# A decode kernel with two attention layers: parts of three query weight blocks loaded through the GpSimd queue onto chosen partitions

## The chip, the cores and the metric

The kernel runs on one core of a Trainium2 chip. The metric is the time on the device in microseconds; three runs of the kernel before gave 1343.22, 1343.85 and 1345.13, so the median is 1343.85.

## The reference

One token of width 640 goes through an attention layer with a key and value cache, a two-layer MLP, and then through both again with the same weights and the same cache.

```python
B, Sq, D = 1, 1, 640
H, Sk, Dh = 32, 8192, 128
def _A_ref(x, k_cache, v_cache, wq, wo):
    q = (lambda x, *d: x.transpose(*d))((x @ wq).reshape(B, Sq, H, Dh), 0, 2, 1, 3)
    scores = jnp.einsum("bhqd,bhkd->bhqk", q, k_cache) * (Dh ** -0.5)
    p = _softmax(scores, axis=-1)
    o = jnp.einsum("bhqk,bhkd->bhqd", p, v_cache)
    return (lambda x, *d: x.transpose(*d))(o, 0, 2, 1, 3).reshape(B, Sq, H * Dh) @ wo
...
x = x + _A_ref(_layernorm(x, axis=-1), A_k_cache, A_v_cache, A_wq, A_wo)
x = x + _B_ref(_layernorm(x, axis=-1), B_w1, B_w2)
x = x + _A_ref(_layernorm(x, axis=-1), A_k_cache, A_v_cache, A_wq, A_wo)
x = x + _B_ref(_layernorm(x, axis=-1), B_w1, B_w2)
```

All data are float32. Each of the 32 heads has 4 MB of keys and 4 MB of values, and both attention layers read them all, apart from a few pieces that stay on the chip between the layers.

## The kernel before

The work is a stream of loads. The keys and values are cut into units of up to 6 MB (`UNITS`, laid out in host memory in `kv` in the order of `ORDER`), and each unit is one transfer over all 128 partitions from SyncE's queue into `ring`, a buffer of 34,000 columns in which `place` looks for room. `pump` (L179) issues the next units while there is room, and is called each time that `release` gives a piece back, which is after the last matmul that reads it. So SyncE issues a load when PE has finished with an older one, and two to three loads are always queued ahead of PE.

PE, VectorE and ScalarE work head by head: scores (L516), the largest of them (L531, L536, L537), the exponentials (L545), four transposes (L552), values (L570), and the sum over the blocks (L587 to L604). Four heads are a group, eight groups a layer. In layer 2 the heads run in another order (`HEADS[1]`). Inside the program the layers are `L` = 0 and 1; this text calls them layer 1 and layer 2. Groups are counted by `k` from 0.

Between the pieces of a head's scores and values `side_work` slips in steps of two queues, `chores` and `slow`. A generator there says for which engine its next step is. Two of them matter here. `run_out(k)` is queued when group k + 1 begins; it projects the outputs of group k with `wo` and then calls `load_wo`, which fetches from ScalarE's queue (L280) the output weights of group k + 1 and the query weights of group k + 2 in one transfer of 2560 KB into `both_t`: 2560 columns of query weights, five row blocks of 512, and 2560 of output weights. `queries_of(k + 1)` is queued with the third head of group k; it runs `wide_queries` (L435): five matmuls (L440), one for each block of 128 of the 640 rows, that spread over four strips of the array, and then for each of the four heads a row scaled by VectorE (L452) and one matmul that sums the strips (L454). So the query weights are asked for with the first head of a group and used with its third.

The order of the instructions on each engine is that in which the Python code emits them (`manual_schedule`); waits between engines and for transfers are put in by the framework from what each instruction reads and writes. Transfers from one kind of queue share eight semaphores in turn, so that a ninth transfer waits for the first to be complete.

At the end of layer 1 the next layer's first units are placed in `mix`, `wct` and the region `by_parts` (`ring` beyond the units, L142), which holds `w2` at the end of each layer; the last loads of a layer are parts of `w2`. The buffer `by_parts` has 4480 columns; between the ends of the layers units reach 2880 columns into it, and the other 1600 lie unused.

Of the kernel before, what the change touches and what calls it, by code (L numbers as in the profile page):

```python
# [10 lines left out]
F32 = mybir.dt.float32  # L11
# [4 lines left out]
P = 128  # L16
D = 640
H = 32
SK = 8192
DH = 128  # L20
DFF = 1728
EPS = 1e-5
NB = D // P
HG = 4
NG = H // HG
# [62 lines left out]
RING = 4248  # L88
WC_AT = [5, 8]
MIX_AT = [[7, 9, 11, 13], [12, 16, 20, 24]]  # L90
FLAT = 3072
EDGE = 4096
BIG = 1536
# [30 lines left out]


@with_exitstack
def decode_kernel(ctx: ExitStack, tc: tile.TileContext, x, kv, wq, wo, wqo, w1, w2, out):
    nc = tc.nc
    consts = ctx.enter_context(tc.tile_pool(name="consts", bufs=1))
    wts = ctx.enter_context(tc.tile_pool(name="wts", bufs=1))  # L130
# [7 lines left out]

    ring = consts.tile([P, 8 * (RING + W2_UNITS)], F32, name="ring")
    by_parts = ring[:, 8 * RING :]  # L142
# [8 lines left out]
    dram_at, o = {}, 0  # L151
# [119 lines left out]
    wo_t = both_t[:, HG * D :].rearrange("p (j d) -> p j d", d=D)  # L271

    def load_wq(g, queue):
        queue.dma_start(both_t[:, : HG * D], wq[P * g : P * g + P])

    def load_wo(L, k, queue):

        g = GROUPS[L][k]
        if 0 < k < NG - 1:
            queue.dma_start(both_t, wqo[L, k - 1])  # L280
# [132 lines left out]
    def queries(g, xc, r):  # L413

        pq = side
        for c in range(NB):
            for j in range(HG):
                nc.tensor.matmul(
                    pq[32 * j : 32 * j + 32, :DH],
                    xc[:, c : c + 1].to_broadcast([P, 32]),  # L420
                    wq_t[:, c, j * DH : (j + 1) * DH],
                    start=(c == 0),
                    stop=(c == NB - 1),
                )
        yield "dve"
        row = work.tile([P, DR], F32, name="q_row")[:, :DH]
        nc.vector.tensor_scalar(row, pq[:, :DH], r[0], SCALE, op0=ALU.mult, op1=ALU.mult)
        yield "pe"
        pt = side
        nc.tensor.matmul(pt[:, :HG], row, sel[:, :HG], start=True, stop=True)  # L430
        yield "dve"
        qT[g] = work.tile([P, HG], F32, name="qT", bufs=2)
        nc.vector.tensor_copy(qT[g], pt[:, :HG])

    def wide_queries(g, xc, r):  # L435

        pq = side
        for c in range(NB):
            strip = c % 4
            nc.tensor.matmul(  # L440
                pq[32 * strip : 32 * strip + 32],
                xc[:, c : c + 1].to_broadcast([P, 32]),
                wq_t[:, c],
                start=c < 4,
                stop=c in (1, 2, 3, 4),
                skip_group_check=True,
            )
# [246 lines left out]
    def attention_and_mlp(L, xr, s, before=None):  # L694
# [25 lines left out]
                    queue.pop(0)  # L720

        def queries_of(k):
            yield from wide_queries(groups[k], xc, r)

        def run_out(k):

# [51 lines left out]
        def due(h):  # L778
# [105 lines left out]
    def mlp(L, o, last, xp, ph):  # L884
# [128 lines left out]
        for c in range(NB):  # L1013
# [1 line left out]
            nc.tensor.matmul(  # L1015
                pq[32 * g : 32 * g + 32, :DH],
                cols[:, c : c + 1].to_broadcast([P, 32]),
                wq_t[:, c, (HG - 1) * DH :],
                start=c < 4,
                stop=c in (1, 2, 3, 4),  # L1020
                skip_group_check=True,
# [44 lines left out]
def _laid_out(A_x, A_k_cache, A_v_cache, A_wq, A_wo, B_w1, B_w2):  # L1066
# [24 lines left out]
    wq = np.asarray(A_wq).reshape(NB, P, NG, HG * DH).transpose(2, 1, 0, 3).reshape(NG, P, HG * D)  # L1091
    wo = np.asarray(A_wo)[:, _COLS].reshape(NG, HG, DH, D).transpose(0, 2, 1, 3)
    wqo = [
        [np.concatenate([wq[b], wo[a].reshape(P, HG * D)], 1) for a, b in zip(gs[1:-1], gs[2:])]
        for gs in GROUPS
# [16 lines left out]
                for loads in W2_LOADS  # L1112
            ]
        ),
    }


# [22 lines left out]
```

## Time and profile before

| What | Value |
|---|---|
| Median of three runs | 1343.85 us |
| Span of the profiled execution, from the first to the last instruction | 1340.6 us |
| Between the span and the median | 3.25 us |
| TensorE matmul busy | 874.0 us, 65% |
| VectorE busy | 290.2 us, 22% |
| ScalarE busy | 62.6 us, 5% |
| GpSimd busy | 2.9 us, 10 instructions |
| Read from memory | 570.83 MB, 426 GB/s over the span |

The page lists of the profiled execution its span; the time around it is taken as the difference to the median of the runs. The lines of the page that matter are shown in the prediction. In a line of the page's fifth part stand the line of the program, the engine, the operation, output and input, how often; then busy time in us and the mean of one in ns; then the idle time of the engine just before, and what ended it. In a window's line the last two numbers are the mean busy share of the 16 DMA engines and what they moved.

### The profile page before, as it was taken

How to read it: one execution, taken by the hardware profiler on the slowest of the kernel's cores; microseconds unless marked ns; L12 is line 12 of the kernel's file. 1: busy time of each engine (PE TensorE's matmuls, PEld its weight loads, DVE VectorE, ACT ScalarE, POOL GpSimd, SP SyncE). 2: the span in 40 equal slices, each digit the busy share in tenths (PEclk: the TensorE clock that was granted, in tenths of full speed). 3: DMA queues.
4: the chain of work that ended last, by engine and by line, in shares of the span. 5: the costliest groups of instructions: out<-in, count | busy, mean ns of one | idle time of the engine just before them, and what ended most of it. 6: DMA issues, size and time to landing. Idle time of an engine off the chain costs nothing.

```text
span 1340.6 us, 13403 instructions
## 1 busy us (share of the span) xinstructions
PE 874.0 (65%) x5806; PEld 255.5 (19%) x5806; DVE 290.2 (22%) x956; ACT 62.6 (5%) x155; POOL 2.9 (0%) x10
## 2 busy tenths in 40 slices
PE   5463575767657656676688755657566666567687
PEld 2110121111111111112243211112111111111123
DVE  2120121211212112223123212221221212212222
ACT  0000000000000000000000000000000000000000
POOL 0000000000000000000000000000000000000000
PEclk8686787988777887788799977887778787888789
DMA  9999999999999999999999999999999999999998
GB/s 395 431 435 430 442 423 437 429 428 437 432 434 429 428 439 426 433 425 415 425 396 425 430 435 433 432 433 431 433 429 434 432 428 433 437 427 436 425 424 333
DMA packets 24546, 571.70 MB, mean 426 GB/s; under 512 B 2724, under 2 KB 2984, under 8 KB 6952
## 3 DMA queue, kind: packets, MB, share of 16 engines
q1 hardware_dynamic: 21464, 529.31, 92.1%
q10 hardware_dynamic: 3024, 41.53, 7.3%
q8 instruction: 46, 0.75, 0.2%
q14 instruction: 12, 0.10, 0.0%
HBM read 570.83 MB, written 0.00 MB: 426 GB/s over the span
## 4 chain that ended last, share of the span: by engine, by line
DMA 67%; PE 27%; DVE 4%; ACT 1%; issue 1%; SPq 0%; ACTq 0%; DVEq 0%
DMA ring<-in_kv 66%; PE ps L516 10%; PE outs L570 9%; PE side L672 1%; DMA ring<-in_w 1%; DVE p L591 1%; PE acc L621 1%; PE side L440 1%; ACT p L545 1%; DVE h_t L531 1%; PE small L536 1%; PE small L604 1%; PE side L454 1%; DVE p L552 0%; DVE h_t L537 0%
## 5 line engine op out<-in xcount | busy, mean ns | idle before, releaser
L516 PE MATMUL ps<-ring,spread_q 128*32 128x512 f32 (+3 forms) x2088 | 332.7, 727 | 149.2 <-DMA ring<-in_kv 148.6
L570 PE MATMUL outs<-ring,p 128*4 128x512 f32 (+3 forms) x2080 | 310.6, 732 | 164.1 <-DMA ring<-in_kv 95.7
L531 DVE TENSOR_REDUCE h_t<-ps 128x1 f32<-128x512 f32 x64 | 44.3, 691 | 365.4 <-PE ps L516 365.4
L570 PEld LDWEIGHTS outs<-ring,p 128*4 128x4 f32 x2080 | 50.6, 95 | 348.4 <-issue 233.8
L516 PEld LDWEIGHTS ps<-ring,spread_q 128*32 128x32 f32 x2088 | 63.9, 124 | 277.5 <-issue 188.8
L545 ACT ACTIVATE p<-ps,h_t 128x512 f32<-128x512 f32 x63 | 43.3, 687 | 1161.2 <-DVE h_t L537 1161.2
L552 DVE STREAM_TRANSPOSE p<-p 128x128 f32<-128x128 f32 x256 | 79.8, 312 | 63.9 <-ACT p L545 57.2
L587 DVE TENSOR_SCALAR p<-outs,ind 128x128 f32<-128x128 f32 x64 | 22.5, 351 | 317.2 <-PE outs L570 317.2
L604 PE MATMUL small<-ones,p 128*128 128x1 f32 (+1 forms) x128 | 25.3, 267 | 97.4 <-DVE p L591 97.4
L591 DVE SCALAR_TENSOR_TENSOR p<-outs,ind,p 128x128 f32<-128x128 f32 x188 | 66.0, 351 | 6.7
L536 PE MATMUL small<-ident,h_t 128*128 128x128 f32 x128 | 32.7, 339 | 40.1 <-DVE h_t L531 39.9
L604 PEld LDWEIGHTS small<-ones,p 128*128 128x128 f32 x128 | 19.9, 195 | 159.7 <-DVE p L591 158.9
L672 PE MATMUL side<-w_t,wct 128*128 128x448 f32 (+1 forms) x80 | 45.3, 651 | 0.0
L452 DVE TENSOR_SCALAR q_row<-side,ln_r 128x128 f32<-128x128 f32 x56 | 19.5, 349 | 106.0 <-PE ps L516 59.0
L440 PE MATMUL side<-both_t,ln_xc 128*32 128x512 f32 x140 | 37.3, 844 | 0.0
L536 PEld LDWEIGHTS small<-ident,h_t 128*128 128x128 f32 x128 | 20.0, 196 | 89.0 <-DVE h_t L531 85.5
L621 PE MATMUL acc<-both_t,o_cols 128*64 128x320 f32 x220 | 34.6, 458 | 0.0
L454 PEld LDWEIGHTS side<-sel,q_row 128*128 128x128 f32 x112 | 19.3, 216 | 56.3 <-DVE q_row L452 29.9
L537 DVE TENSOR_REDUCE h_t<-small 128x1 f32<-128x128 f32 x64 | 18.7, 292 | 35.4 <-PE small L536 35.4
L454 PE MATMUL side<-sel,q_row 128*128 128x1 f32 x112 | 24.1, 284 | 0.3 <-DVE q_row L452 0.2
L621 PEld LDWEIGHTS acc<-both_t,o_cols 128*64 128x64 f32 x220 | 15.5, 147 | 29.4 <-issue 17.7
L672 PEld LDWEIGHTS side<-w_t,wct 128*128 128x128 f32 x80 | 13.5, 211 | 32.4 <-issue 32.4
(148 smaller groups left out, 219.5 us busy)
## 6 DMA issues: line engine op xcount, KB each, us to landing
ring<-in_kv SPq DMA_DIRECT2D x50, 6144.0 KB, 35.0
ring<-in_kv SPq DMA_DIRECT2D x23, 4096.0 KB, 33.2
ring<-in_kv SPq DMA_DIRECT2D x29, 2048.0 KB, 27.7
both_t<-in_wqo ACTq DMA_DIRECT2D x12, 2560.0 KB, 24.7
ring<-in_kv SPq DMA_DIRECT2D x4, 5120.0 KB, 34.6
ring<-in_kv SPq DMA_DIRECT2D x9, 1024.0 KB, 23.9
w_t<-in_w ACTq DMA_DIRECT2D x1, 4320.0 KB
ring<-in_kv SPq DMA_DIRECT2D x5, 768.0 KB, 29.5
```

Of the source, the lines that this page charges most:

```text
L440: nc.tensor.matmul(pq[32 * strip : 32 * strip + 32], xc[:, c : c + 1].to_broadcast([P, 32]), wq_t[:, c], start=c < 4, stop=c in (1, 2, 3, ...
L454: nc.tensor.matmul(mine[:, :1], row, one_of_each, start=True, stop=True, skip_group_check=True)
L516: nc.tensor.matmul(hd.ps[32 * g : 32 * g + 32, c : c + n], spread_q[:, 3 - r : 35 - r], tile_of[:, at + g * n : at + (g + 1) * n], start=f ...
L531: nc.vector.tensor_reduce(hd.nm, hd.ps, AX.X, ALU.max, negate=True)
L536: nc.tensor.matmul(pt[:, :P], hd.nm.to_broadcast([P, P]), ident, start=True, stop=True)
L545: nc.scalar.activation(hd.p, hd.ps, AF.Exp, bias=hd.low, scale=scale, accum_out=hd.l)
L552: nc.vector.transpose(hd.all_p[:, b * P : (b + 1) * P], hd.p[:, b * P : (b + 1) * P])
L570: nc.tensor.matmul((hd.out if r0 < 2 else hd.out_2)[32 * g : 32 * g + 4, r0:r1].rearrange("p r d -> p (r d)"), hd.all_p[:, 32 * i : 32 * i ...
L591: nc.vector.scalar_tensor_tensor(oc, hd.out[:, r], ind[:, r : r + 1], oc, op0=ALU.mult, op1=ALU.add)
L604: nc.tensor.matmul(pt[:, :n], part, mask.to_broadcast([P, n]), start=i == 0, stop=i == len(parts) - 1,)
L621: nc.tensor.matmul(acc[64 * g : 64 * g + 64, : 2 * DR], col.to_broadcast([P, 64]), wt[:, 2 * DR * g : 2 * DR * (g + 1)], start=first, stop ...
L672: nc.tensor.matmul(pt[:, :n], wct[:, c], w1_t[:, c, f : f + n], start=(c == 0), stop=(c == NB - 1),)
```

## The change

Three pieces of query weights leave the transfer of `load_wo` and come through the GpSimd queue instead: two of five row blocks (3 and 4) of the weights that are loaded at k = 2, in both layers, and one row block (4) of those loaded at k = 4 in layer 2. A row block is 128 rows of 512 columns, 256 KB. The other transfer from ScalarE's queue starts at a later column and is shorter by as much; to that end the row blocks are stored in the order 3, 4, 0, 1, 2 (`POS`).

The rows that leave are laid on some of the partitions only: 0 to 11, 16 to 19, 28 to 31, 32 to 43, 48 to 51, 60 to 67, 92 to 99 and 124 to 127 for the first, and a part of these for the second. Each such partition holds up to five rows (`slots`) of 512 columns beside each other. A slot is 520 columns wide, and the slots take the first 1024 (or 512) columns of `both_t`, which is now the end of `ring`, and the unused columns of `by_parts` ahead of it. That area is set to zero once at the start.

The table `loads` lists the transfers: the number of DMA engines each is meant to use, the first partition, the number of partitions, and the slots; with 0 slots it moves a few words into the unused columns between slots. The access patterns are cut so that the outermost sizes of both sides have that number as common divisor. The numbers of one round, 3, 1, 1, 2, 1, 1, 6, 1, add up to 16.

For the matmul the rows of a slot need the matching elements of the normalized input as a column. `early_columns`, queued as a slow step with head 4 of each layer, makes these columns: two matmuls bring blocks 3 and 4 of the input into rows, VectorE sets a row in `mix` to zero and copies the pieces to their places, five or eight matmuls turn them into columns, and one copy keeps them in `early_x`. `wide_queries` then has three or four matmuls of the ordinary kind, and five or three with a slot as weights and the column of `early_x`; elements for partitions that hold no such row are zero.

```diff
+POS = {4: 0, 3: 1, 0: 2, 1: 3, 2: 4}
+SLOT = HG * DH + 8
+GAP = 64
+EARLY = {
+    2: dict(
+        chunks=[3, 4],
+        slots=5,
+        held=[
+            (5, [(0, 12), (16, 4), (28, 4), (48, 4), (60, 8), (92, 8), (124, 4)]),
+            (3, [(32, 12)]),
+        ],
+        loads=[
+            (3, 0, 12, 5),
+            (1, 12, 4, 0),
+            (1, 16, 4, 5),
+            (2, 20, 8, 0),
+            (1, 28, 4, 5),
+            (1, 96, 4, 5),
+            (6, 68, 24, 0),
+            (1, 92, 4, 5),
+            (3, 32, 12, 3),
+            (1, 12, 4, 0),
+            (1, 48, 4, 5),
+            (2, 20, 8, 0),
+            (2, 60, 8, 5),
+            (6, 68, 24, 0),
+            (1, 124, 4, 5),
+        ],
+    ),
+    4: dict(
+        chunks=[4],
+        slots=3,
+        held=[
+            (3, [(0, 12), (16, 4), (28, 4), (60, 8), (92, 4)]),
+            (2, [(32, 12), (96, 4)]),
+        ],
+        loads=[
+            (3, 0, 12, 3),
...
+            (7, 68, 28, 0),
+        ],
+    ),
+}
+EARLY_IN = [[2], [2, 4]]
...
-    both_t = wts.tile([P, 2 * HG * D], F32, name="both_t")
+    both_t = ring[:, both_at:]
...
+    def load_early(L, k):
+
+        spec = EARLY[k]
+        for i, load in enumerate(spec["loads"]):
+            engines, first, rows, slots = load
+            pieces, n = split(load)
...
+            source = early[o:o_end].rearrange("(g m) -> g m", g=pieces)[:, :n]
+            where = slots_of(spec)[first : first + rows]
...
+            nc.gpsimd.dma_start(where, source)
...
-            queue.dma_start(both_t, wqo[L, k - 1])
+            n = HG * DH * len(EARLY[k]["chunks"]) if k in EARLY_IN[L] else 0
+            queue.dma_start(both_t[:, n:], wqo[L, k - 1, :, n:])
+            if k in EARLY_IN[L]:
+                load_early(L, k)
             return
...
+    nc.vector.memset(ring[:, both_at - 8 * 200 : both_at], 0.0)
...
-    def wide_queries(g, xc, r):
+    def wide_queries(g, xc, r, k=None):
 
         pq = side
-        for c in range(NB):
+        parts = [(xc[:, c : c + 1], wq_t[:, POS[c]]) for c in range(NB)]
+        if k in early_x:
+            spec = EARLY[k]
+            parts = [p for c, p in enumerate(parts) if c not in spec["chunks"]]
+            parts += [
+                (early_x[k][:, s : s + 1], slots_of(spec)[:, s, : HG * DH])
+                for s in range(spec["slots"])
+            ]
+        for c, (column, weights) in enumerate(parts):
...
+            if where == 4:
+                slow.append([early_columns(L, xc), "pe"])
```

On PE, in layer 1, the third head of group 2 computes the queries of group 3, whose weights are the first to come in two parts. Before:

```order
L604 MATMUL small<-ones,p 128x1 [waits DVE_49]
L516 MATMUL ps<-ring,spread_q 32x512 [waits DMAHW6_49,PE_49]
L516 MATMUL ps<-ring,spread_q 32x512 x3
L440 MATMUL side<-both_t,ln_xc 32x512 [waits DMAHW4_49,Activation_49]
L440 MATMUL side<-both_t,ln_xc 32x512 x4
L516 MATMUL ps<-ring,spread_q 32x512 x4
L454 MATMUL side<-sel,q_row 128x1 [waits DVE_49]
```

The same place with the change, where the line numbers have moved (L613 was L440, L689 was L516):

```order
L777 MATMUL small<-ones,p 128x1 [waits DVE_49]
L689 MATMUL ps<-ring,spread_q 32x512 [waits DMAHW6_49,PE_49]
L689 MATMUL ps<-ring,spread_q 32x512 x3
L613 MATMUL side<-ring,ln_xc 32x512 [waits DMAHW4_49,Activation_49]
L613 MATMUL side<-ring,ln_xc 32x512 x2
L613 MATMUL side<-ring,early_x 32x512 [waits DMASW5_49,DMASW6_49,DMASW4_49,DMASW7_49,DMASW2_49,DMASW0_49]
L613 MATMUL side<-ring,early_x 32x512 x4
L689 MATMUL ps<-ring,spread_q 32x512 x4
L627 MATMUL side<-sel,q_row 128x1 [waits DVE_49]
```

Two of the five query matmuls have gone, and five come behind the other three; the first of these waits for transfers of the GpSimd queue (DMASW), ahead of the head's remaining scores. On GpSimd, which before had only the four powers of the layer norms, these transfers stand for k = 2 in layer 1:

```order
L461 TENSOR_TENSOR ln_r<-ln_v,mhalf 128x1 [waits DVE_49]
L392 DMA ring<-in_early 12x5x512 [waits DMAHW5_49,DMAHW4_49,PE_49]
L392 DMA ring<-in_early 4x3x4
L392 DMA ring<-in_early 4x5x512
L392 DMA ring<-in_early 8x1x4
L392 DMA ring<-in_early 4x5x512 x2
L392 DMA ring<-in_early 24x1x4
L392 DMA ring<-in_early 4x5x512
L392 DMA ring<-in_early 12x3x512 [waits DMASW0_49]
L392 DMA ring<-in_early 4x3x4 [waits DMASW1_49]
L392 DMA ring<-in_early 4x5x512 [waits DMASW2_49]
L392 DMA ring<-in_early 8x1x4 [waits DMASW3_49]
```

The first eight follow each other without a wait; from the ninth on each waits until an earlier one is complete. On VectorE, the steps of `early_columns` in layer 1 come behind the two of `run_out(0)`:

```order
L906 RECIPROCAL rl_g<-small 128x4 [waits PE_49]
L907 SCALAR_TENSOR_TENSOR o_cols<-o_cols,rl_g 128x4 [waits DVE_49]
L578 MEMSET mix 32x640
L587 COPY mix<-side 32x5x12 [waits DVE_49,PE_49]
L587 COPY mix<-side 32x5x4 x3
L587 COPY mix<-side 32x5x8 x2
L587 COPY mix<-side 32x5x4
L587 COPY mix<-side 32x3x12
L594 COPY early_x<-side 128x5 [waits PE_49]
L704 TENSOR_REDUCE h_t<-ps 128x1 [waits PE_49]
```

Before, the largest of the scores (L531, now L704) followed at once.

More of the change, by code (lines that the diff above doesn't have):

```diff
@@ new lines, with placed, filled @@
+EARLY_IN = [[2], [2, 4]]
+def placed(spec):
+    o = 0
+    for slots, runs in spec["held"]:
+        n = sum(m for _, m in runs)
+        for first, m in runs:
+            yield slots, first, m, o, n
+            o += m
+        o += (slots - 1) * n
+def filled(spec):
+    at = np.full((spec["slots"], P), -1)
+    for slots, first, m, o, n in placed(spec):
+        for s in range(slots):
+            for i in range(m):
+                c, d = divmod(o + s * n + i, P)
+                at[s, first + i] = P * spec["chunks"][c] + d
+    held = np.sort(at[at >= 0])
+    assert (held == np.concatenate([P * c + np.arange(P) for c in spec["chunks"]])).all()
+    loaded = np.zeros((spec["slots"], P), bool)
+    for _, first, rows, slots in spec["loads"]:
+        loaded[:slots, first : first + rows] = True
+    assert loaded[at >= 0].all()
+    return at
@@ L91, with split @@
+def split(load):
+    engines, _, rows, slots = load
+    pieces = engines if engines > 1 else slots or 3
+    n = rows * (slots * HG * DH if slots else 12 if engines == 1 else 4)
+    return pieces, n // pieces
+EARLY_AT, _o = {}, 0
+for _L in range(2):
+    for _k in EARLY_IN[_L]:
+        for _i, _load in enumerate(EARLY[_k]["loads"]):
+            EARLY_AT[_L, _k, _i] = _o
+            _pieces, _n = split(_load)
+            _o += _pieces * (_n + GAP)
+EARLY_SIZE = _o
 FLAT = 3072
@@ L722, in queries_of @@
         def queries_of(k):
-            yield from wide_queries(groups[k], xc, r)
+            yield from wide_queries(groups[k], xc, r, k - 1)
         def run_out(k):
@@ L1090, in _laid_out @@
     w2[W2_LAST:, -1, : D // 2] = w2[:W2_LAST, -1, D // 2 :]
-    wq = np.asarray(A_wq).reshape(NB, P, NG, HG * DH).transpose(2, 1, 0, 3).reshape(NG, P, HG * D)
+    order = sorted(POS, key=POS.get)
+    wq = np.asarray(A_wq).reshape(NB, P, NG, HG * DH)[order].transpose(2, 1, 0, 3).reshape(NG, P, HG * D)
+    early = np.zeros(EARLY_SIZE, wq.dtype)
+    for k, spec in EARLY.items():
+        at = filled(spec)
+        for L in (L for L in range(2) if k in EARLY_IN[L]):
+            cols = HG * DH * GROUPS[L][k + 1]
+            rows = np.zeros((spec["slots"], P, HG * DH), wq.dtype)
+            rows[at >= 0] = np.asarray(A_wq)[at[at >= 0], cols : cols + HG * DH]
+            for i, load in enumerate(spec["loads"]):
+                _, first, count, slots = load
+                if slots:
+                    pieces, n = split(load)
+                    block = early[EARLY_AT[L, k, i] :][: pieces * (n + GAP)].reshape(pieces, n + GAP)
+                    held = rows[:slots, first : first + count].transpose(1, 0, 2)
+                    block[:, :n] = held.reshape(pieces, n)
     wo = np.asarray(A_wo)[:, _COLS].reshape(NG, HG, DH, D).transpose(0, 2, 1, 3)
@@ L1114, in _laid_out @@
         ),
+        "early": early,
     }
```

76 lines of the change are left out of this document (67 added, 9 removed).

## The prediction

> **What bounds the kernel now.** I read the page first: the span, the DMA slices, the queues, the chain that ended last and the two largest groups of PE.
>
> ```profile
> span 1340.6 us, 13403 instructions
> ...
> DMA  9999999999999999999999999999999999999998
> GB/s 395 431 435 430 442 423 437 429 428 437 432 434 429 428 439 426 433 425 415 425 396 425 430 435 433 432 433 431 433 429 434 432 428 433 437 427 436 425 424 333
> ...
> q1 hardware_dynamic: 21464, 529.31, 92.1%
> q10 hardware_dynamic: 3024, 41.53, 7.3%
> q8 instruction: 46, 0.75, 0.2%
> ...
> DMA 67%; PE 27%; DVE 4%; ACT 1%; issue 1%; SPq 0%; ACTq 0%; DVEq 0%
> ...
> L516 PE MATMUL ps<-ring,spread_q 128*32 128x512 f32 (+3 forms) x2088 | 332.7, 727 | 149.2 <-DMA ring<-in_kv 148.6
> L570 PE MATMUL outs<-ring,p 128*4 128x512 f32 (+3 forms) x2080 | 310.6, 732 | 164.1 <-DMA ring<-in_kv 95.7
> ```
>
> The reader is to see that the 16 DMA engines are busy from end to end (92.1 + 7.3 + 0.2 = 99.6% of their time) at some 430 GB/s, and that PE waits for ring data 148.6 + 95.7 = 244 us in all. So added PE or DVE work is covered as long as it stays far below that, and time falls only if the engine that finishes last has less to move. The slice with 333 GB/s is the last one, so next I cut the end into windows (busy time of the engines, PE clock, then the DMA share and GB/s).
>
> ```profile
> core 0: us, PE busy (x) PEld busy (x) DVE busy (x) ACT busy (x) POOL busy (x), PEclk, DMA share, GB/s
> 1330.00:1331.00 1.00, 1.00 (x8) 0.94 (x8) 0.61 (x4) 0.37 (x2) 0.00 (x0) 1.00 1.00 399
> 1331.00:1332.00 1.00, 0.74 (x21) 0.63 (x25) 0.17 (x1) 0.00 (x0) 0.00 (x0) 1.00 0.83 334
> 1332.00:1333.00 1.00, 1.00 (x36) 0.96 (x32) 0.00 (x0) 0.00 (x0) 0.00 (x0) 1.00 0.58 242
> 1333.00:1334.00 1.00, 1.00 (x30) 0.71 (x20) 0.08 (x2) 0.00 (x0) 0.00 (x0) 1.00 0.59 242
> 1334.00:1335.00 1.00, 0.99 (x26) 0.76 (x25) 0.87 (x6) 0.00 (x0) 0.00 (x0) 1.00 0.49 197
> 1335.00:1336.00 1.00, 0.81 (x19) 0.59 (x15) 0.23 (x3) 0.00 (x0) 0.15 (x1) 1.00 0.37 133
> 1336.00:1337.00 1.00, 0.96 (x28) 0.39 (x20) 0.00 (x0) 0.00 (x0) 0.40 (x1) 1.00 0.02 8
> ```
>
> A share of 0.58 is 9.3 of 16 engines. Seven engines run out at about 1331.6 (the 0.17 missing in that window is 2.7 us of engine time, 0.4 us for each of seven); nine go on, the last to about 1336.3. The sum of what is missing from 1331 to 1336.3 is 0.17 + 0.42 + 0.41 + 0.51 + 0.63 + 0.28 = 2.4 us of all engines: more than that, less the cost of small pieces, no redistribution can win there. The change's table names seven engines that get weights (0 to 2, 4, 7, 8, 15) and passes over nine, so the count fits. The q8 row shows instruction fetches as one load that need not be even: 0.2% of 16 engines is 43 us, 4.8 us each on nine. The page doesn't name the engines.
>
> Layer 1 has the same unevenness, seen where the queue runs dry.
>
> ```profile
> 636.00:637.00 1.00, 0.00 (x0) 0.00 (x0) 0.00 (x0) 0.00 (x0) 0.00 (x0) 1.00 0.80 302
> 637.00:638.00 1.00, 0.94 (x16) 0.42 (x16) 0.00 (x0) 0.00 (x0) 0.00 (x0) 1.00 0.91 272
> ...
> 690.00:693.00 3.00, 2.23 (x24) 1.39 (x24) 0.88 (x3) 0.37 (x1) 0.00 (x0) 1.00 0.88 359
> 693.00:694.00 1.00, 1.00 (x12) 0.92 (x15) 0.50 (x4) 0.37 (x2) 0.00 (x0) 1.00 0.85 223
> 694.00:695.00 1.00, 1.00 (x33) 0.96 (x36) 0.17 (x1) 0.00 (x0) 0.00 (x0) 1.00 0.74 280
> ```
>
> Missing here: 0.20 + 0.09 + 0.36 + 0.15 + 0.26 = 1.06 us.
>
> **The change, part by part.** *Bytes moved between engines.* In layer 1 512 KB of weights leave the even load, in layer 2 768 KB. Each engine loses a sixteenth, 32 and 48 KB. At 430/16 = 27 GB/s that is 1.2 and 1.8 us. Seven engines get the bytes back in pieces of 2 KB: 256 in layer 1, 388 in layer 2 (132 for the third block, four of them spare). The nearest rate for small rows is the window from 1335 (rows of 1.25 to 5 KB): 133/(0.37·16) = 22.5 GB/s, so 91 ns a piece against 76 ns at full rate. In layer 2 each of the seven carries 52 to 64 pieces, 4.7 to 5.8 us, less the 1.8 removed: 2.9 to 4.0 later. The seven then end at about 1331.6 + 2.9 = 1334.5 to 1335.6, the nine at 1336.3 − 1.8 = 1334.5. The end comes 0.7 to 1.8 us earlier; I take **−1.4**, where most of the seven meet the nine. In layer 1 the bound from above is the 1.06 us that is missing, from below nothing, since part of it is waiting for the issue of the next load; I take **−0.7**.
>
> *PE and DVE.* The next rows price the added work.
>
> ```profile
> L440 PE MATMUL side<-both_t,ln_xc 128*32 128x512 f32 x140 | 37.3, 844 | 0.0
> ...
> 1.84 0.48 DVE L323 MEMSET outs<- 128x512 f32 x1
> ...
> 6.66 0.32 DVE L1041 TENSOR_REDUCE x_s<-xr 128x1 f32<-128x160 f32 x1 [4.24 <-DMA xr<-in_x]
> ```
>
> One pass of a query matmul costs 37.3/140 = 0.27 us. Two passes each, three matmuls more for a group with five slots: 1.6 us twice; two more for the third block: 1.1 us. The columns for them (7 and 10 short matmuls, 8 and 14 small DVE copies) come once a layer. All of it lies in PE's 244 us of waiting and costs **0**; without that cover it would be some 8 us. The memset of 1600 columns, 1.5 us by the row of 512, fits into the 4.24 us for which DVE waits for `x`.
>
> *Small transfers and their reports.* 42 transfers on a queue that the kernel didn't use, seventeen of them only to move the choice of engine on. No row prices their reports; below by nothing, above by the 91 ns of a 2 KB piece for each on each engine, 42 · 0.09 = 3.8 us. Most are a few bytes, so I take **+0.2**, and one more instruction fetch may add to one engine, +0.2 on average.
>
> *The wait that is added.* The query matmul of a group now waits for the early pieces, and everything of PE stands behind it. When do they land?
>
> ```profile
> ring<-in_kv SPq DMA_DIRECT2D x50, 6144.0 KB, 35.0
> ...
> both_t<-in_wqo ACTq DMA_DIRECT2D x12, 2560.0 KB, 24.7
> ...
> 205.14 0.33 ACTq L280 DMA_DIRECT2D both_t<-in_wqo  x1
> ...
> 247.64 1.45 PE L440 MATMUL side<-both_t,ln_xc 128*32 128x512 f32 x9
> ...
> 846.49 0.33 ACTq L280 DMA_DIRECT2D both_t<-in_wqo  x1
> ...
> 883.90 2.37 PE L440 MATMUL side<-both_t,ln_xc 128*32 128x512 f32 x9
> ...
> 1011.23 0.34 ACTq L280 DMA_DIRECT2D both_t<-in_wqo  x1
> ...
> 1055.58 2.77 PE L440 MATMUL side<-both_t,ln_xc 128*32 128x512 f32 x9
> ```
>
> The time from issue to use is 42.5, 37.4 and 44.4 us. A ring row of 48 KB takes an engine 1.8 us, a weight row of 20 KB 0.76 us. The weights alone would need 6 us but land after 24.7: 8 · (1.8 + 0.76) = 20.6 us and the ends. So an engine alternates between the two queues row by row, and the price of the new queue is its number of turns, 1.8 us each. If a turn takes all that one transfer has for an engine, there are 15 transfers and so some 17 turns: nine beside the weights at 2.6 us, eight at 1.9, 39 us, about on time. A PE that comes 4 us late costs nothing, because loads are queued:
>
> ```profile
> 244.87 25.77 DMA ring<-in_kv
> ...
> 257.00 0.33 SPq L189 DMA_DIRECT2D ring<-in_kv  x1
> ...
> 863.95 40.46 DMA ring<-in_kv
> ...
> 887.64 0.33 SPq L189 DMA_DIRECT2D ring<-in_kv  x1
> ```
>
> The load issued at 244.87 lands at 270.6, and SP's next issue, which PE releases, comes at 257.0: 11.6 us of slack with 2 us for a start (904.4 − 887.6 − 2 = 14.8 in layer 2). Landings up to some 53 us after issue cost **0**. I take this case, being nearest to the 24.7 us row.
>
> Sum: −1.4 − 0.7 + 0.4 = −1.7 us on the span of 1340.6. The median of the runs, 1343.85, is 3.25 above the span, and that part stays: **1342.1 us**.
>
> **Rivals.** *Two pieces or one to a turn (slower).* If the new queue gives an engine one piece of 2 KB a turn, the engines with 40 pieces need 40 + 15 = 55 turns, 23 + 46 · 1.9 = 110 us; two at a time 35 turns, 73 us. PE then stands at the query until the ring queue is empty and the pieces have the engines alone. From 53 us on each group costs idle DMA. In layer 1 the queue is empty at 270.6; PE then takes 9.4 us (257.0 − 247.6) to the next release and the load 2 us to start: 11. In layer 2: 3.7 + 2, 6. Two at a time: +17, **1359 us** (the third block, 14 to 24 turns, is still in time). One at a time: the third block costs some 9 as well (between the other two), and in each of the three some 25 pieces are still left (2.3 us) and the second batch, which waits for the first one's reports, has to start (2 us), 4 each: 17 + 9 + 12 = +38, **1380 us**. For it speaks the row-by-row turn of the other queues; against it that those rows are whole rows, and the trace has no transfer of many pieces. The Trainium skill, "DMA: Bandwidth & Descriptors", section "Queues, rings and completion order", says that an engine drains a whole packet, typically 9 to 17 descriptors, before it changes rings; by that the forecast holds. The same page's section "SWDGE vs HWDGE vs iDMA" has a packet preferably at most 4096 B, which would be two pieces and 1359 us. No row here decides between them.
>
> *Other engines than named (no effect, or slower).* If the pieces are dealt to all engines, nothing is gained and 644 · 15 ns / 16 = 0.6 us lost: **1344 us**; if they fall on late engines, 2.9 us and 1.7 us are added: 1348. For it: the engine follows only from the order of the transfers. Against: the counts 3+1+1+2+1+1+6+1 make 16. The Trainium skill, same page, section "Why a DMA increments its semaphore by 16 and not by 1", tells of such an exception for some direct copies of that queue.
>
> **Numbers.** Forecast (right engines, in time) 0.55, own range 1340.6 to 1343.6. Other engines 0.10, two pieces a turn 0.15, one piece 0.20. The range takes in all but the last: 1340.6 to 1361. A measurement here tells about 0.2%, 2.7 us. Faster (below 1341.2): 0.15, the good end of the forecast. Within: 0.40 of the forecast and 0.05 of the other engines, 0.45. Slower: 0.40.
>
> **What would show it.** Right: in the last windows the DMA share stays near 1 until some 1334 and falls within 2 us; the early pieces' matmul follows the three others of its group with under 5 us of idle PE; no DMA slice in either layer drops below 400 besides the first and the last. Wrong: a wait of PE of 20 us or more at the query with DMA windows near 0 behind it (pieces per turn), or shares of 0.58 for 4 us at the end as now (engines).

## The result, and the profile after

The changed kernel takes 1395.71 us, the median of four runs (1392.38 to 1400.56); the kernel before takes 1343.96 us. The ratio is 1.039, with a 95% interval of 1.0368 to 1.0412. The prediction, 1342.1 us with a range up to 1361, was wrong.

The profiled execution took 1396.84 us. These are its lines on the page:

```profile
span 1395.1 us, 13619 instructions
...
DMA  9999999769999999999999999969999979999997
GB/s 398 434 435 431 428 425 424 316 262 431 432 428 441 427 436 426 432 426 418 429 388 429 430 430 431 424 248 403 432 429 427 426 308 434 433 430 433 429 424 328
DMA packets 28883, 571.75 MB, mean 410 GB/s; under 512 B 6738, under 2 KB 6998, under 8 KB 11288
...
q1 hardware_dynamic: 21464, 529.31, 88.9%
q0 software_dynamic: 4336, 1.36, 0.4%
q10 hardware_dynamic: 3024, 40.22, 6.8%
...
L613 PE MATMUL side<-ring,early_x 128*32 128x512 f32 x26 | 9.1, 1059 | 77.7 <-DMA ring<-in_early 77.7
```

Four slices of the DMA row have fallen (316 and 262, 248, 308 GB/s), in three places, and PE waits 77.7 us for the early pieces. The timeline has PE's three waits in brackets, with their ends in the first column, and SyncE's first load after the first of them:

```profile
280.21 2.74 PE L613 MATMUL side<-ring,early_x 128*32 128x512 f32 x9 [32.26 <-DMA ring<-in_early]
...
291.83 9.31 SPq L287 DMA_DIRECT2D ring<-in_kv  x2
...
937.83 2.74 PE L613 MATMUL side<-ring,early_x 128*32 128x512 f32 x9 [27.47 <-DMA ring<-in_early]
1117.67 1.07 PE L613 MATMUL side<-ring,early_x 128*32 128x512 f32 x3 [17.93 <-DMA ring<-in_early]
```

In windows (busy times, then PE's granted clock, DMA share and GB/s), first around each wait and then within the first:

```profile
260.00:300.00 40.00, 16.05 (x92) 4.67 (x96) 5.32 (x17) 0.78 (x2) 3.32 (x5) 0.66 0.46 181
920.00:950.00 30.00, 10.07 (x56) 3.25 (x60) 3.60 (x11) 0.78 (x2) 3.33 (x5) 0.61 0.47 178
1110.00:1130.00 20.00, 10.23 (x48) 2.82 (x48) 3.60 (x11) 0.78 (x2) 0.00 (x0) 0.59 0.60 237
...
270.00:275.00 5.00, 0.00 (x0) 0.00 (x0) 0.00 (x0) 0.00 (x0) 2.60 (x4) 0.50 0.13 22
280.00:285.00 5.00, 4.79 (x24) 1.39 (x28) 0.35 (x1) 0.00 (x0) 0.00 (x0) 0.62 0.00 0
285.00:290.00 5.00, 3.12 (x23) 1.15 (x22) 2.10 (x6) 0.78 (x2) 0.00 (x0) 1.00 0.01 2
```

The idle DMA time is 40 · 0.54 = 21.6, 30 · 0.53 = 15.9 and 20 · 0.40 = 8.0 us, 45.5 us in all. In layer 1 the loads that were queued have run out soon after 270; the last pieces land at 280, and PE, whose clock has fallen to 0.50 while it waited, needs until 291.8 to release the next load. The rest is in the queues' shares: q1, q10, q0 and q8 (0.2%) are 96.3% of 1395.1 us = 1343.5 us, and were 99.6% of 1340.6 = 1335.2. So 45.5 us idle and 8.3 us more of work make 53.8 of the 54.5 us by which the span grew.

GpSimd's timeline shows that it asked early. The transfers of k = 2 in layer 1 start at 165.27, as soon as the previous queries are done, while the ordinary weights are asked for 40 us later:

```profile
165.27 2.92 POOL L392 DMA_DIRECT2D ring<-in_early  x4 [154.55 <-PE ps L689]
189.83 0.72 POOL L392 DMA_DIRECT2D ring<-in_early  x1 [21.63 <-issue]
...
271.27 2.60 POOL L392 DMA_DIRECT2D ring<-in_early  x4 [19.08 <-issue]
275.83 0.72 POOL L392 DMA_DIRECT2D ring<-in_early  x1 [1.96 <-issue]
```

From the first issue to PE's start it is 280.21 − 165.27 = 115 us here, and by the same rows 110 us in layer 2 (issue at 827.42) and 102 us for the third block (1015.66). Between its issues GpSimd stands for up to 23.6 us for nothing that the profile names.

### The profile page after: what moved, and what is told of

Same layout as the page of the kernel before. It is cut to its first block, busy times and chain, and to the rows that moved or that the text cites. A ratio compares the mean times of both kernels' runs of the same rounds, so it can differ in the third digit from the quotient of the medians.

```text
span 1395.1 us, 13619 instructions
## 1 busy us (share of the span) xinstructions
PE 885.5 (63%) x5856; PEld 261.1 (19%) x5856; DVE 295.8 (21%) x984; ACT 62.5 (4%) x155; POOL 31.1 (2%) x52
## 2 busy tenths in 40 slices
DMA packets 28883, 571.75 MB, mean 410 GB/s; under 512 B 6738, under 2 KB 6998, under 8 KB 11288
## 3 DMA queue, kind: packets, MB, share of 16 engines
q1 hardware_dynamic: 21464, 529.31, 88.9%
q0 software_dynamic: 4336, 1.36, 0.4%
## 4 chain that ended last, share of the span: by engine, by line
DMA 48%; PE 26%; issue 17%; DVE 4%; another core or an unknown queue 2%; POOL 1%; ACT 1%; SPq 0%; ACTq 0%; POOLq 0%; DVEq 0%
DMA ring<-in_kv 44%; PE outs L743 10%; PE ps L689 9%; PE side L613 2%; DMA ring<-in_wqo 1%; DVE p L764 1%; POOL ring L392 1%; DMA ring<-in_w 1%; DVE h_t L704 1%; PE side L845 1%; ACT p L718 1%; PE small L709 1%; PE acc L794 1%; PE small L777 1%
## 5 line engine op out<-in xcount | busy, mean ns | idle before, releaser
L743 PE MATMUL outs<-ring,p 128*4 128x512 f32 (+3 forms) x2080 | 318.1, 748 | 158.4 <-DMA ring<-in_kv 92.5
L689 PE MATMUL ps<-ring,spread_q 128*32 128x512 f32 (+3 forms) x2104 | 330.6, 714 | 117.6 <-DMA ring<-in_kv 117.1
L704 DVE TENSOR_REDUCE h_t<-ps 128x1 f32<-128x512 f32 x64 | 44.3, 691 | 336.2 <-PE ps L689 336.2
L689 PEld LDWEIGHTS ps<-ring,spread_q 128*32 128x32 f32 x2104 | 65.5, 123 | 248.1 <-issue 179.1
L625 DVE TENSOR_SCALAR q_row<-side,ln_r 128x128 f32<-128x128 f32 x56 | 19.5, 349 | 184.3 <-PE side L613 75.9
L613 PE MATMUL side<-ring,early_x 128*32 128x512 f32 x26 | 9.1, 1059 | 77.7 <-DMA ring<-in_early 77.7
L777 PEld LDWEIGHTS small<-ones,p 128*128 128x128 f32 x128 | 19.5, 192 | 157.8 <-DVE p L764 156.9
L392 POOL DMA_DIRECT2D ring<-in_early x42 | 28.2, 674 | 589.1 <-PE ps L689 332.6
L794 PE MATMUL acc<-ring,o_cols 128*64 128x320 f32 x220 | 35.6, 469 | 0.0
L613 PE MATMUL side<-ring,ln_xc 128*32 128x512 f32 x130 | 33.9, 838 | 0.0
L627 PE MATMUL side<-sel,q_row 128*128 128x1 f32 x112 | 24.5, 288 | 0.4 <-DVE q_row L625 0.2
```

Source lines behind the costliest of these rows:

```text
L613: nc.tensor.matmul(pq[32 * strip : 32 * strip + 32], column.to_broadcast([P, 32]), weights, start=c < 4, stop=c >= len(parts) - 4, skip_gr ...
L627: nc.tensor.matmul(mine[:, :1], row, one_of_each, start=True, stop=True, skip_group_check=True)
L689: nc.tensor.matmul(hd.ps[32 * g : 32 * g + 32, c : c + n], spread_q[:, 3 - r : 35 - r], tile_of[:, at + g * n : at + (g + 1) * n], start=f ...
L704: nc.vector.tensor_reduce(hd.nm, hd.ps, AX.X, ALU.max, negate=True)
L743: nc.tensor.matmul((hd.out if r0 < 2 else hd.out_2)[32 * g : 32 * g + 4, r0:r1].rearrange("p r d -> p (r d)"), hd.all_p[:, 32 * i : 32 * i ...
L777: nc.tensor.matmul(pt[:, :n], part, mask.to_broadcast([P, n]), start=i == 0, stop=i == len(parts) - 1,)
```

## Experiments

Three explanations stood at the start. **T**: PE stops at the query because the pieces come a small packet at a time, each packet behind a row of 48 KB. **W**: the added matmuls, copies and columns cost. **Q**: the GpSimd queue or its bytes cost by themselves. All ratios are to the kernel before on the same chip.

**No early pieces.** The early transfers go, and with them the matmuls and columns that use them. What stays of the change is the order of the row blocks, the layout and the memset.

```diff
-EARLY_IN = [[2], [2, 4]]
+EARLY_IN = [[], []]
...
-            if where == 4:
+            if where == 4 and EARLY_IN[L]:
```

> No transfer on the GpSimd queue, no columns for them and full weight transfers; the order of the row blocks, both_t as the end of ring and the memset stay. Theory T (PE stands at three queries for early pieces that land too late, and the ring queue runs dry behind it): 1343 to 1346 us, as before the change. Rival W (the rest of the change costs: memset, the moved buffer, other semaphores): above 1350. Rival Q (any traffic on the GpSimd queue slows the stream): as T.

Measured: 1343.33 us, ratio 0.9997 (0.9988 to 1.0006). What is left of the change costs nothing. This kernel does without the added matmuls, copies and columns, so it can't decide on W; the two short sets below do.

**The same blocks in one transfer.** They come through GpSimd's queue, each set as one transfer over all partitions, and are read by ordinary matmuls.

```diff
...
-            if k in EARLY_IN[L]:
-                load_early(L, k)
+            if n:
+                nc.gpsimd.dma_start(both_t[:, :n], wqo[L, k - 1, :, :n])
```

> The same three pieces of weights come through the GpSimd queue, but each as one transfer over all 128 partitions to their old place, read by the ordinary matmuls. Theory T: eight rows of 2 or 4 KB and a report for each engine are some 10 turns, so they land within about 25 us, PE does not wait, 1343 to 1347 us, no balance gained. Rival Q: the new queue beside the stream costs whatever its transfers are, above 1355.

Measured: 1344.08 us, ratio 1.0004 (0.9995 to 1.0013). The queue as such costs nothing, so Q falls. Its rows, from the page's queues and from the DMA issues:

```profile
q0 software_dynamic: 368, 1.31, 0.2%
...
ring<-in_wqo POOLq DMA_DIRECT2D x2, 512.0 KB, 17.1
```

Three transfers give 3 · 16 = 48 reports; the other 320 packets carry 1.31 MB, 4.1 KB each. Of 512 KB an engine gets 32 KB, eight such packets and a report; nine turns beside rows of 1.8 us are 16 us, and 17.1 were measured. So a turn is a packet of 4096 B. In the two transfers of 512 KB that is one row of a partition; in the third, of 256 KB, and in the changed kernel (322 packets for 644 pieces, below) it is two rows of 2 KB. The section "SWDGE vs HWDGE vs iDMA" of the Trainium skill's page "DMA: Bandwidth & Descriptors" has a packet of preferably at most 4096 B, and the trace agrees. The 9 to 17 descriptors of that page's section "Queues, rings and completion order" would be 18 KB or more here, which it doesn't bear out.

**One part of the change at a time.** The two sets at k = 2 alone, and the third block alone.

```diff
-EARLY_IN = [[2], [2, 4]]
+EARLY_IN = [[2], [2]]      # the first of the two kernels
+EARLY_IN = [[], [4]]       # the second
```

> The third block (k = 4 in layer 2) undone: 30 transfers instead of 42, two stalls instead of three. Theory T: the third stall goes, 18 us of PE waiting and about 8 us of idle DMA, so 1384 to 1388 us. Rival Q by the number of transfers: 1344 + 52 x 30/42 = 1381.

> Only the third block comes early, 12 transfers and one stall. Theory T: 8 us of idle DMA and 1 to 2 us of longer packets, 1352 to 1355 us. Rival Q by the number of transfers: 1344 + 52 x 12/42 = 1359.

Measured: 1386.09 us, 1.0315 (1.0301 to 1.0329), and 1350.94 us, 1.0054 (1.004 to 1.0067). The costs, 42.6 and 7.5 us, add up to nearly that of the change, 51.8; the second time is a little below what was expected. The queue's rows on the two pages:

```profile
q0 software_dynamic: 3424, 1.08, 0.3%
```

```profile
q0 software_dynamic: 912, 0.28, 0.1%
```

0.28 MB are some 68 packets of 4096 B, and 12 transfers make 192 reports. 912 is far more, but it is 16 · 57, and 3424 is 16 · 214, or 107 for each set of 15 transfers. In the changed kernel itself 6738 − 2724 = 4014 more packets than before are under 512 B, so only 322 of the 4336 carry pieces; reports are 42 · 16 = 672. The trace's records of this queue have the sizes: 322 packets of 4096 B, 672 of 4 B, 3070 of 8 B and 272 of 16 to 192 B. The reading that fits: whatever the number of engines that get data, each of the 16 engines gets as many packets as the busiest one, the others tiny ones. The table `loads` then gives these very counts: for each transfer half of the pieces of its busiest engine and one report, and for a transfer of a few words two packets. That is 8 · 11 + 7 + 6 · 2 = 107 and 6 · 7 + 5 + 5 · 2 = 57 turns.

The records also show when the turns pass. Of the 16 · 107 = 1712 packets of the first set in the changed kernel, 919 start in the 100 us up to 265, beside the rows of the ring; the other 793 start in the 15 us after that, when the ring's queue has run dry.

**Is it the wait or the traffic?** In the first of the next two kernels all three places use the table of the third block (one row block each). The second has the same 36 transfers, asked for 6 to 15 us later, into columns that nobody reads; the weights come whole in the ordinary transfer, and the added matmuls and columns are gone.

```diff
     2: dict(
-        chunks=[3, 4],
-        slots=5,
+        chunks=[4],
+        slots=3,
...
# the second kernel, besides
-        end = both_at + HG * DH * len(spec["chunks"])
+        end = both_at
...
+        gate = work.tile([P, HG], F32, name="gate")
+        nc.gpsimd.tensor_copy(gate, qT[GROUPS[L][k]])
```

> All three places use the short table of the third block: one row block each, 12 transfers, about 57 turns of an engine instead of 107 at the first two. Theory T (the cost is PE's wait at the query for pieces that come one small packet at a time between rows of 48 KB): each place lands at about 105 to 112 us after the issue if GpSimd is held up as in the changed kernel, at some 65 to 75 us with 57 turns; either way after the use at 78 to 80 us or only just before, so between 0 and 8 us for each place, as the third block alone cost 7 us: 1352 to 1368 us, with less idle DMA at the first two places (0 to 10 us each) than in the changed kernel (22 and 16). Rival W (the cost is the added matmuls, copies and columns): about 1344 plus a constant for every group, three times that of the third block alone, 1366. Rival Q (bytes on the GpSimd queue cost by themselves): in proportion to 0.75 MB, 1373.

> The same 36 transfers (12 at each of three places, issued by GpSimd at about the same moment) into columns that nobody reads; the weights come whole in the ordinary transfer, so this moves 0.75 MB more than the kernel with three short sets. Theory T (only PE's wait stops the stream): no wait of PE at the query, no stretch of idle DMA, 1344 to 1349 us: 0.75 MB more are 1.8 us at 430 GB/s, and the small packets some 1 to 3 us. Rival (the small packets themselves hold the DMA engines up, whoever reads them): as long as the kernel with three short sets, within 2 us.

Measured: 1359.36 us, 1.0109 (1.0094 to 1.0125), read; 1346.73 us, 1.0021 (1.0012 to 1.003), unread. Some 13 of the 16 us go when nobody reads the pieces, so the traffic is a small part. By the trace's records the 16 DMA engines are idle for 16.4 us in the first of the two executions and for 3.6 in the second; that is nearly all of the difference between them, 13.4 us, and fits T. In the unread kernel the end of layer 2 could also be seen without a stall:

```profile
1334.00:1335.00 1.00, 0.74 (x16) 0.61 (x19) 0.17 (x1) 0.00 (x0) 0.00 (x0) 1.00 0.96 402
...
1336.00:1337.00 1.00, 1.00 (x31) 0.73 (x24) 0.00 (x0) 0.00 (x0) 0.00 (x0) 1.00 0.90 365
1337.00:1338.00 1.00, 1.00 (x28) 0.95 (x30) 0.64 (x4) 0.00 (x0) 0.00 (x0) 1.00 0.79 318
1338.00:1339.00 1.00, 0.98 (x22) 0.57 (x15) 0.49 (x4) 0.00 (x0) 0.00 (x0) 1.00 0.64 228
1339.00:1340.00 1.00, 0.92 (x24) 0.44 (x20) 0.05 (x1) 0.00 (x0) 0.56 (x1) 1.00 0.07 24
```

0.04 + 0.10 + 0.21 + 0.36 = 0.7 us are missing before the share falls to nothing, where 2.4 were: the pieces do go to engines that are idle at the end. What this wins isn't shown, since here the ordinary transfer still brings the weights whole.

**Does every microsecond of the wait cost?** The short table at k = 2 in both layers, nothing at the third place.

```diff
# against the kernel with three short sets
-EARLY_IN = [[2], [2, 4]]
+EARLY_IN = [[2], [2]]
```

> The short table at k = 2 of both layers, read, and nothing at the third place. PE waited 10 and 12 us at these two queries in the kernel with three short sets. Theory T with the prediction's slack (a PE that comes up to some 10 to 12 us late costs little, since loads are queued): no stretch of idle DMA over 2 us at either place, and 1345 to 1349 us, which is the two sets' small packets. Rival (every us that PE waits is lost): 1343.5 + 22 = 1365 us. If the three places of that kernel cost alike: 1354 us.

Measured: 1348.62 us, 1.004 (1.0025 to 1.0055). PE's wait in layer 1, and the windows behind it:

```profile
258.66 1.08 PE L610 MATMUL side<-ring,early_x 128*32 128x512 f32 x3 [8.30 <-issue]
```

```profile
260.00:265.00 5.00, 5.00 (x26) 1.31 (x23) 0.70 (x2) 0.00 (x0) 0.00 (x0) 0.54 1.00 433
265.00:270.00 5.00, 2.90 (x20) 0.78 (x20) 2.89 (x9) 0.78 (x2) 0.00 (x0) 0.80 0.81 346
270.00:275.00 5.00, 5.00 (x26) 1.21 (x26) 0.16 (x1) 0.00 (x0) 0.00 (x0) 0.52 0.83 295
```

The profile names no cause for this wait; for the one of 9.4 us in layer 2, at the same matmul, it names the transfer of the pieces. The wait of 8.3 us leaves 5 · 0.19 + 5 · 0.17 = 1.8 us of idle DMA; behind that of 9.4 us no window of 5 us falls below a share of 0.95. So the slack that the prediction worked out is there, a little shorter than it said (11.6 us in layer 1). This also settles W: the kernel has the added matmuls, copies and columns in both layers, and by the records its DMA engines are idle for 6.0 us in all, where it was 4.7 before. With three short sets the third place waited 19.5 us and lost (1 − 0.49) · 15 = 7.6 us (window 1075 to 1090, share 0.49).

**Turns or transfers?** If GpSimd's pauses set the pace, the price goes by transfers, not by packets. Both variants are cut from the unread kernel. The first drops the transfers with 0 slots; the second keeps all 12, but a transfer with weights brings one slot only.

```diff
-            (1, 12, 4, 0),      # first variant, and the other four like it
...
-            (3, 0, 12, 3),      # second variant, and the other six like it
+            (3, 0, 12, 1),
```

> The kernel whose early pieces nobody reads, without the transfers of a few words between the others: 8 transfers at each place, not 12; the bytes of weights stay. Theory T (a small packet, a turn of 1.8 us, on every engine for each packet of the busiest engine and one for the report): the transfers left out had 1 to 3 turns each, so 57 turns become some 47, and the whole set takes some 85 us from the first issue to the last landing where the kernel with the moves took 101 in layer 1. Rival P (GpSimd held up ahead of each transfer sets the pace, so a price for each transfer): 8/12 of 101, 67 us. The time moves little either way, 1344 to 1347 us.

> The same kernel with all 12 transfers, but each data transfer brings one slot and not two or three: a third of the bytes, the same number of transfers and of reports. Theory T: 2 packets on the busiest engine (1 where it has 4 rows) and the report, so some 31 turns, 57 us from the first issue to the last landing in layer 1. Rival P (a price for each transfer): 12 transfers still, about 100 us. The time 1343 to 1346 us.

The first variant has seven transfers in a place, not eight. For the unread kernel and the two variants in turn: the packets of the page, first and last issue in layer 1 on GpSimd's timeline, and from the DMA issues in 160 to 300 us the last transfer's time from issue to landing. (In the second fence that row is the median of two transfers of 48 KB; the last one alone has 56.2.)

```profile
q0 software_dynamic: 2736, 0.84, 0.3%
...
178.04 3.41 POOL L392 DMA_DIRECT2D ring<-in_early  x5
...
244.75 0.59 POOL L392 DMA_DIRECT2D ring<-in_early  x1 [11.58 <-DMA ring<-in_early]
...
ring<-in_early POOLq DMA_DIRECT2D x1, 0.4 KB, 34.2
```

```profile
q0 software_dynamic: 2256, 0.83, 0.2%
...
175.27 2.83 POOL L382 DMA_DIRECT2D ring<-in_early  x4
...
203.06 0.68 POOL L382 DMA_DIRECT2D ring<-in_early  x1 [10.14 <-issue]
...
ring<-in_early POOLq DMA_DIRECT2D x2, 48.0 KB, 56.3
```

```profile
q0 software_dynamic: 1296, 0.31, 0.1%
...
178.29 4.67 POOL L391 DMA_DIRECT2D ring<-in_early  x8
...
210.26 0.56 POOL L391 DMA_DIRECT2D ring<-in_early  x1 [9.50 <-DMA ring<-in_early]
...
ring<-in_early POOLq DMA_DIRECT2D x1, 0.4 KB, 24.5
```

| kernel | transfers a place | q0 packets / 48 = turns | first issue to last landing | a turn |
|---|---|---|---|---|
| all, unread | 12 | 57 | 244.75 + 34.2 − 178.04 = 100.9 us | 1.77 us |
| no moves | 7 | 47 | 203.06 + 56.2 − 175.27 = 84.0 us | 1.79 us |
| one slot | 12 | 27 | 210.26 + 24.5 − 178.29 = 56.5 us | 2.09 us |

The time goes by turns: theory T gave 85 and 57 us (for 31 turns in the last kernel, which has 27), the price by transfers 59 (for seven) and 100. GpSimd's pauses without a named cause don't set this pace: they are 124.5 us in all in the unread kernel and 1.1 us with one slot, and the turn is no shorter there. In the changed kernel they are 235.4 us. In turn, one slot, unread and changed:

```profile
POOL ring L391 <- issue: 1.1, 3, 0.5
```

```profile
POOL ring L392 <- issue: 124.5, 14, 15.7
```

```profile
POOL ring L392 <- issue: 235.4, 16, 23.6
```

One run of each variant took 1354.43 and 1350.31 us, above what was expected (up to 1347 and 1346). The first was run again, unchanged; why the second was slow stays open.

> The kernel without the transfers of a few words once more, timed: its one look took 1354.4 us where the kernel with them took 1346.7. Theory T with the choice of engines by order (without those transfers the same weights fall on other engines, some of which end late anyway): 1352 to 1356 us. Rival (that look was an outlier): 1345 to 1348 us.

Measured: 1352.19 us, 1.0068 (1.0051 to 1.0085). So the transfers of a few words matter: without them the same weights cost 5.5 us more than with them. The two pages show where that goes, first with these transfers (the unread kernel), then without.

```profile
span 1344.5 us, 13473 instructions
...
q1 hardware_dynamic: 21464, 529.31, 91.9%
```

```profile
span 1350.5 us, 13450 instructions
...
q1 hardware_dynamic: 21464, 529.31, 91.9%
```

The same 529.31 MB of SyncE's queue keep the engines busy for 91.9% of 1344.5 = 1235.6 us and of 1350.5 = 1241.1 us. So most of the difference is longer rows. The end of layer 2 is a smaller part: the share falls slowly, 0.88, 0.73, 0.48, 0.29, 0.12 from 1341 to 1346, 2.5 us missing where 0.7 were with these transfers. The pieces no longer fall on the early engines, which is the prediction's rival of other engines; the longer rows are not in it.

**The same aim without that queue.** One row block at k = 2 of both layers (first kernel), and at the third place as well (second), by one transfer of ScalarE's queue onto 33 partitions, 80 us before its use.

```diff
+    k: dict(chunks=[4], slots=4, held=[(4, [(0, 32)])], loads=[(3, 0, 33, 4)])
...
-            nc.gpsimd.dma_start(where, source)
+            nc.scalar.dma_start(where.rearrange("p s m -> p (s m)"), source)
...
+            if k in EARLY_IN[L]:            # in queries_of, behind the queries
+                load_early(L, k)
```

> A try at what the change is after without its queue: at k = 2 of both layers one row block (256 KB) comes by one transfer from ScalarE's queue, onto 33 partitions with four slots side by side, issued right after the previous queries, about 80 us before its use. Theory T: rows of 8 KB on three engines, 11 to 12 turns, land some 30 us after the issue, so no wait of PE at the query and no idle DMA there. Each engine loses 16 KB (0.6 us) and three get 88 KB back (3.3 us): if these three are among the seven that end early, the end of layer 2 comes 0.6 us earlier and that of layer 1 up to 0.6: 1342.3 to 1343.5 us; if they are not, up to 2.7 us later in each layer, 1349. Rival (any transfer that lies on part of the engines stalls PE as in the changed kernel): 1355 or more.

> The same with the third place of layer 2 as well, on the same three engines: these then carry 2 times 88 KB less 32 KB, 5.3 us more, in layer 2, and would end at about 1336.9 on the scale of the kernel before instead of 1331.6, the others at 1335.1. Theory T: no wait of PE, no idle DMA at the three places; the end of layer 2 0.6 us later than before, that of layer 1 up to 0.6 earlier: 1343 to 1345 us. Rival (any transfer on part of the engines stalls PE): 1360 or more.

Measured: 1348.82 us, 1.0034 (1.0022 to 1.0045), and 1351.77 us, 1.0056 (1.0044 to 1.0069). PE no longer waits at the query, so the rival falls; but no gain came. T allowed 1349 us for the first only if the three engines were late ones, and missed the second by 7 us. Two windows of the first kernel show where it lost, while the block comes and at the end of layer 1. Behind them stand the same stretch of the kernel before and the turn of the layers in the second kernel.

```profile
190.00:195.00 5.00, 3.40 (x21) 0.92 (x18) 2.29 (x7) 0.78 (x2) 0.00 (x0) 1.00 0.97 374
...
710.00:712.00 2.00, 2.00 (x14) 0.70 (x10) 0.12 (x1) 0.00 (x0) 0.00 (x0) 0.50 0.01 5
```

```profile
190.00:195.00 5.00, 3.40 (x21) 1.00 (x14) 2.29 (x7) 0.78 (x2) 0.00 (x0) 1.00 1.07 462
```

```profile
710.00:720.00 10.00, 8.71 (x110) 3.44 (x106) 4.33 (x15) 0.87 (x2) 0.00 (x0) 1.00 1.00 420
```

The engines are busy but move less: q1, the same 529.31 MB, takes 92.0% of 1348.2 us = 1240.3 us, where it took 92.1% of 1340.6 = 1234.7. By the records, rows of 48 KB that start from 180 to 200, while the block comes, take 2.05 us on average and 1.82 in the kernel before. At the turn of the layers PE also works at a clock of 0.50 in this execution, and the queue runs dry for 2 us. The second kernel has the same block in layer 1 and no such gap, so the block alone doesn't explain it. Why the rows become longer was not tried; one guess, not shown, is that several engines write to the same partitions.

No kernel with such pieces beat the kernel before.

## Why the prediction was wrong

**The step that failed is "The wait that is added".** It said: "If a turn takes all that one transfer has for an engine, there are 15 transfers and so some 17 turns", 39 us, and took the wait at 0. Two things were wrong in it. A turn is one packet of 4096 B (one transfer per set, 17.1 us). And the turns don't belong to the engine's own data: a transfer meant for three engines or one gives all sixteen as many packets as its busiest one. With 57 to 107 turns at 1.8 us a set can't land in the 80 us between the previous queries and its use; 107 turns would be 193 us, and nearly half of them came only because PE's stop emptied the other queue. That the engines' turns are those of the busiest one is read from the packet counts, which the table gives for the long and the short set, and from the landing times of three kernels. The kernel with one slot has 27 turns where this reading gave 31, which stays open, and what the packets of 8 B are for isn't shown.

**The use and the issue.** The prediction put the issue with that of the ordinary weights, at 205 us. GpSimd issued at 165, 40 us earlier, which made the wait shorter than the same turns from 205 would have.

**The slack** (landings up to 53 us after that issue cost nothing) held roughly: waits of 8.3 and 9.4 us left some 2 us of idle DMA.

**PE and DVE work, 0**: held as far as can be seen. No kernel has this work without the transfers, but with two short sets idle DMA time grew by 1.3 us in all, the waits for the pieces included. The memset and the layout cost nothing.

**Balance, −1.4 and −0.7.** The choice of engines worked: with pieces that nobody waits for, the missing share at the end of layer 2 falls from 2.4 to 0.7 us. That this shortens the time isn't shown by any run, and what it gives in layer 1 wasn't read apart.

**Small transfers, +0.2**: too small. q0 is busy for 0.4% of 1395.1 = 5.6 us, q10 gives back 97.9 − 94.9 = 3.0, and q1 takes 5.5 us more. Unread, the three short sets cost 3.2 us in all; some 1.8 us of that is an estimate for 0.75 MB of weights that come twice, at 430 GB/s. So even in time the pieces would have eaten up a good part of the 2.1 us that they were to win.

**The rivals.** "One at a time" had the right mechanism of the stop: PE stands until the ring queue is empty. That its landing also fits, 110 us against 115, 110 and 102, is luck: it counted 55 turns from an issue at 205, and there were 107 (57 for the third block) from an issue 40 us earlier. Its reason, one piece a turn, was wrong, and its sum of 38 us too small: idle times of 11, 6 and 9 us and 12 for the rest against 21.6, 15.9 and 8.0. In layer 1 the pieces land 10 us after the queue ran dry, not 4, and PE takes 291.8 − 280.2 = 11.6 us to the next release, not 9.4, its clock being 0.50 and 0.62 at first. The 8.3 us of longer DMA work come on top. Its chance of 0.20, left outside the range, was too small for a term that no row priced and whose worst case was 38 us. "Two pieces a turn" had the packet right, but counted only the engine's own.

## What to carry to other kernels

Before a load is cut to chosen DMA engines, count the packets of the whole queue in a profile: if they are 16 times the busiest engine's, each packet of that engine costs one turn behind a row of the other queue, on all engines. An instruction that the next loads hang on must not wait for such a transfer, unless the transfer is asked for earlier than its use by turns times row time. And where one unmeasured term decides between no cost and tens of microseconds, the range has to reach to its far end.

## What the runs showed of the hardware

- By their counts, transfers of GpSimd's queue that are cut to some engines put packets on all 16: 912 for 0.28 MB in 12 transfers, against 368 for 1.31 MB in three over all engines. In the changed kernel 3070 of 4336 packets have 8 B.
- A turn beside rows of 48 KB costs 1.8 to 2.1 us, with packets of 4 to 4096 B (three kernels).
- GpSimd stands between issues, up to 23.6 us and 235.4 us in all, when it issues sets of 107 and 57 such packets an engine; with 27 it is 1.1 us in all.
- PE's granted clock falls to 0.50 while it waits: in the five microseconds after a wait of 32.26 us it was 0.62 on average, after one of 8.3 us still 0.54 in the window 1.3 us later. It was also 0.50 in one window of two microseconds in which PE was busy throughout.
- One transfer of 33 rows of 8 KB, onto 33 partitions, went with a stream of 374 GB/s in one window where it was 462 before, with the engines busy; rows of 48 KB took 2.05 us instead of 1.82.
